# Block attention into a softplus feed-forward: m-tiles of four token tiles instead of three, attention two tiles at a time

## The chip, the core and the metric

The kernel runs on one core of one Trainium2 chip. The time is the device time of one execution in microseconds (us); lower is better. PE is TensorE (its weight loads are shown as PEld), DVE is VectorE, ACT is ScalarE, POOL is GpSimd, and SP is SyncE, which here only issues DMAs. Every engine works through its own instructions in order and waits on semaphores for the others.

## What is computed

Attention within chunks of 64 positions (8 batches, 8 heads, 576 positions, 64 dimensions a head), and on its result, as 4608 tokens of 512 features, a feed-forward layer with softplus and 2048 hidden features:

```python
def _attn_ref(q, k, v):
    B, H, S, D = q.shape
    chunk = 64
    nc = S // chunk
    q_c, k_c, v_c = (t.reshape(B, H, nc, chunk, D) for t in (q, k, v))
    scores = 1.0 / np.sqrt(D) * np.matmul(q_c, k_c.transpose(0, 1, 2, 4, 3))
    scores = scores - np.max(scores, axis=-1, keepdims=True)
    attn = np.exp(scores)
    attn = attn / (np.sum(attn, axis=-1, keepdims=True) + 1e-09)
    return np.matmul(attn, v_c).reshape(B, H, S, D).astype(np.float32)

def _moe_ref(x, w_in, w_out):
    h = x @ w_in
    g = np.maximum(h, 0.0) + np.log1p(np.exp(-np.abs(h)))
    return (g @ w_out).astype(np.float32)
```

The feed-forward's weights come as 64-bit floats, the rest as 32-bit.

## The kernel before

**Tiles.** A token tile is 128 tokens (two chunks, all heads); there are 36. An m-tile is TPM = 3 of them. The hidden features are FC = 16 chunks of 128. A *block* is one m-tile with one chunk: G1 (`gemm1`, L517) multiplies x by a chunk of w_in into PSUM (`ph`), softplus follows on ACT (`sp_g`), and G2 (`gemm2`, L552) multiplies the result by a chunk of w_out and adds it up over the chunks in one PSUM bank (`po`) for each token tile. There are 12 m-tiles, so 192 blocks. Every factor is split into a high and a low part in a format that PE multiplies in one pass, and three products stand for one: G1 has 12 matmuls of 384 columns, G2 9 of 512. `sp_hi` (ACT) and `sp_lo` (DVE) split the softplus; x is split by `att_xh` and `att_xl`.

**Weights.** A *unit* is one chunk of w_in or w_out, 32 in all. Each is loaded as 512 KB of 64-bit floats (`w_load`) and built up from integer halves: `w_top` and `w_low` on ACT, `w_sign` on POOL, `w_shift` and `w_add` on DVE, then the high part (`w_hi`: ACT for w_in, POOL for w_out) and the low part (`w_lo`: DVE for w_in, POOL for w_out and for two units of `LO_POOL`). The first 12 units use 8 places in the space of the second half of w_in, the later ones 3 buffers for the top and 2 for the low part. Three raw buffers take the loads, and the outputs too.

**Order of the m-tiles.** The list `phases` splits the first m-tile: its chunks 0 to 7, then the whole second m-tile, then its chunks 8 to 15. The partial sums of the first half wait in SBUF (`pp`).

**Attention.** Tiles 0 to 5 go one way (T, S, E, V: PE transposes q and k, multiplies, transposes the weights of attention, multiplies by v), tiles 6 to 35 another: q and k are loaded in blocks of 32, transposed by DVE (`blk_t`), and S of tile i and V of tile i - 1 run in one *burst* on PE (`burst`, L509) between a G1 and a G2; DVE, ACT and eight DMAs within SBUF (`blk_swap`) turn the weights of attention in between. Each such tile has 8 DMAs for q, 8 for k, 4 for v and 8 for the swap, all issued by SP. There is one buffer each for q, k, v and the transposed tiles, and one PSUM slot of two banks (`pa`) for bursts.

**Order.** All of it is tasks of a planner (class `Plan`): each has an engine, a cost, the tasks that it needs, an urgency (lower goes first) and the buffers that it takes. The planner runs them through and emits the instructions in that order. G1 and G2 stand in a fixed sequence: G1 of block g, then G2 of block g - LAG, LAG = 2. `BEGIN` lists the first bursts by block. `keep_warm` puts multiplications of the identity where the planner sees a gap of PE before 90 us.

PSUM has 8 banks: 3 `po`, 3 `ph`, 2 for `pa`.

Of the kernel before, what the change touches and what calls it, by code (L numbers as in the profile page):

```python
# [32 lines left out]
class Plan:  # L33
# [12 lines left out]
    def add(self, name, eng, cost, fn, needs=(), urg=0.0, table=None, take=(), kb=0, slack=0.0, after=()):  # L46
        self.tasks[name] = dict(
            name=name, eng=eng, cost=cost, fn=fn, needs=list(needs) + list(after), after=set(after), urg=urg, table=table,
            take=take, kb=kb, slack=slack, seq=len(self.tasks),
        )  # L50

    def order(self):
# [6 lines left out]
        fin, issued, free, tab, dma_free = {}, {}, {}, None, 0.0  # L59
# [29 lines left out]
        while times:  # L89
# [3 lines left out]
            for eng in list(wait):  # L93
# [13 lines left out]
                end = now + cost  # L107
                free[eng] = end
# [26 lines left out]
def chunked_attention_softplus_ffn(  # L135
# [19 lines left out]
    TPM = 3  # L155
# [5 lines left out]
    LAG = 2  # L161
    HALF_FC = 8
    FIRST_BLK = 6
    UW = 512
    RAW_BUFS = 3
    TOP_BUFS = 3
    LOW_BUFS = 2
    FILL = 0.6
# [26 lines left out]
    xs = [  # L195
        tuple(xpool.tile([P, 2 * TPM, KC, C], F32R, name=f"x_{part}{j}") for part in ("hi", "lo"))
        for j in range(2)
    ]

    def x_of(m):  # L200
        return xs[0] if m == 0 else xs[1] if m == 1 else xs[(m + 1) % 2]
# [66 lines left out]
    def w_hi(u, is_in, fc):  # L268
        t, hi, lo = w_parts(u, is_in, fc)
        if is_in:  # L270
            nc.scalar.copy(hi, t)
        else:
            nc.gpsimd.tensor_copy(hi, t)
# [6 lines left out]
    def slot(i, n):  # L280
        if ("slots", i) not in live:
            live["slots", i] = [late.tile([P, DM], F32, name="late") for _ in range(5)]
        return live["slots", i][n]

# [27 lines left out]
    def keep_warm(dst):  # L312
        for _ in range(int(FILL * plan.gap / 0.22)):
            nc.tensor.matmul(dst[:, :P], ident, ident, start=True, stop=True)
        plan.gap = 0.0
# [4 lines left out]
    def pe_t(i):  # L320
        if i < TPM:
            tq, tk = (ps_o.tile([P, DM], F32, name="po") for _ in range(2))
            keep_warm(tq)
        else:
            pa = pa_tile()
            tq, tk = pa[:, 0, :], pa[:, 1, :]
            keep_warm(tq)
# [15 lines left out]
    def pe_s(i):  # L343
        qT, kT = (slot(i, n).rearrange("p (a t) -> p a t", a=HP) for n in (3, 4))
        if i < TPM:
            sc = ps_h.tile([P, 512], F32, name="ph")
            keep_warm(sc)
        else:
            sc = pa_tile()[:, 0, :]
            keep_warm(sc)  # L350
# [12 lines left out]
    def pe_e(i):  # L363
        if i < TPM:
            tp = ps_h.tile([P, 512], F32, name="ph")
            keep_warm(tp)
        else:
            tp = pa_tile()[:, 0, :]
            keep_warm(tp)
# [7 lines left out]
    def pe_v(i):  # L377
        eT, vt = slot(i, 1).rearrange("p (a t) -> p a t", a=HP), hd(slot(i, 2))
        xp = pa_tile()
        keep_warm(xp[:, 0, :])  # L380
        for hp in range(HP):
            for h2 in range(2):
                for c2 in range(2):
# [3 lines left out]
                        xp[o, c2, hp * C : (hp + 1) * C],  # L387
# [5 lines left out]
        live["xp", i] = xp[:, :, : HP * C].rearrange("p c (a t) -> p c a t", t=C)  # L393


    def blk_load(i, name, src):
        dst = ld.tile([P, H, 2, BL], F32, name=name)
# [50 lines left out]
    def blk_v_load(i):  # L448
        v_load(i, ld.tile([P, H * D], F32, name="v"))
# [96 lines left out]
    def sp_lo(w):  # L546
        w["lo"] = g_tile(w, "g_lo")
        nc.vector.tensor_tensor(w["lo"], w["u"], w["hi"].bitcast(F32), op=ALU.subtract)  # L548
# [3 lines left out]
    def gemm2(w):  # L552
        if w["first"]:
            pos[w["ph_no"]] = [ps_o.tile([P, DM], F32, name="po") for _ in range(TPM)]
        g_hi, g_lo, fc = w["hi"], w["lo"], w["fc"]
        w_hi_, w_lo_ = wo[fc]
        if w["first"]:
            keep_warm(pos[w["ph_no"]][0])
        for t in range(TPM):
            ts_ = slice(t * P, (t + 1) * P)  # L560
            for n, (gg, wt) in enumerate(((g_lo, w_hi_), (g_hi, w_lo_), (g_hi, w_hi_))):
                nc.tensor.matmul(  # L562
                    pos[w["ph_no"]][t], gg[:, ts_], wt,
# [3 lines left out]
    parts = {}  # L567

    def evacuate(w, t):
        m, po = w["m"], pos[w["ph_no"]][t]  # L570
        done = w["fc"] == FC - 1
        if done:
            o = ld.tile([P, 2 * UW], I32, name="raw", bufs=RAW_BUFS)[:, :DM].bitcast(F32)
        else:
            o = parts[m, t] = pp.tile([P, DM], F32, name="part")
        if done and (m, t) in parts:
            nc.vector.scalar_tensor_tensor(
                o, po, 1.0 / WSCALE, parts[m, t], op0=ALU.mult, op1=ALU.add
            )
        else:  # L580
            nc.scalar.activation(o, po, AF.Copy, scale=1.0 / WSCALE)  # L581
        live["o", m, t] = o
# [32 lines left out]
    def due(g):
# [3 lines left out]
    units = sorted(  # L619
        [(first_use[fc], 1, fc) for fc in range(FC)] + [(first_use[fc] + 1.5, 0, fc) for fc in range(FC)]  # L620
    )
    of_in, of_out = {}, {}
    for u, (g, is_in, fc) in enumerate(units):
# [4 lines left out]
        if not is_in and fc >= HALF_FC:  # L628
            for j in range(2 * (fc - HALF_FC), min(2 * (fc - HALF_FC) + 2, LATE)):
                users.append("EVVSS"[j % 5] + str(j // 5 + FIRST_BLK - TPM))  # L630
        pl = "DVE" if is_in and u not in LO_POOL else "POOL"
# [167 lines left out]
```

## Time and profile before

| | us |
|---|---|
| median of 3 runs | 901.97 (900.75 to 903.83) |
| profiled execution | 899.45 |
| its span | 897.7 |
| PE busy | 881.9 |
| ACT busy | 392.8 |
| DVE busy | 354.7 |
| POOL busy | 66.8 |
| first G1 starts | 29.41 |
| last matmul ends | 894.02 |

The span is the time from the first to the last instruction that the profiler recorded on the core. In the profile, a line such as L527 is a line of the kernel printed above: L527 are the matmuls of G1, L562 those of G2, L423 and L491 the S and V of the bursts. Waits are put down to the instruction that ended last before the waiting one ran.

### The profile page before, as it was taken

To read this page: it belongs to the slowest core of one execution; us is meant where nothing else is said; L and a number is where in the kernel's file an instruction comes from. 1 tells how busy PE (TensorE), PEld (TensorE's weight loads), DVE (VectorE), ACT (ScalarE), POOL (GpSimd) and SP (SyncE) were. 2 spreads that over 40 slices of the span, in tenths; PEclk is the share of its full clock that TensorE was granted. 3 is DMA by queue.
4 is the path that set the end of the run, shared out by engine and by line. 5 is a ranking of instruction groups with operands and counts; after the bars stand their busy time and mean duration, and the time that the engine had idled before them with its cause. 6 is when DMAs were issued, how large, how long until landed. Compare 5 with 4: busy or idle time off the path is not lost.

```text
span 897.7 us, 16500 instructions
## 1 busy us (share of the span) xinstructions
PE 881.9 (98%) x6490; PEld 789.6 (88%) x6490; DVE 354.7 (40%) x616; ACT 392.8 (44%) x653; POOL 66.8 (7%) x72
## 2 busy tenths in 40 slices
PE   7988999999999999999999999999999999999998
PEld 7877988898898888888888888889889888888997
DVE  4898764233333333333333332332333333331110
ACT  5887556333343343334334334333334334332222
POOL 2656531000000000000000000000000000000000
PEclk9999999999999999999999999999999999999999
DMA  9945552332232223223222222223223222110000
GB/s 241 246 137 176 117 127 62 90 78 48 48 83 48 49 51 71 48 49 74 45 50 72 48 48 69 46 52 76 48 49 83 48 48 48 60 25 1 36 1 35
DMA packets 209501, 63.50 MB, mean 71 GB/s; under 512 B 186896, under 2 KB 202768, under 8 KB 209424
## 3 DMA queue, kind: packets, MB, share of 16 engines
q1 hardware_dynamic: 209424, 62.45, 30.0%
q8 instruction: 51, 0.84, 0.4%
q14 instruction: 26, 0.21, 0.1%
HBM read 45.09 MB, written 9.44 MB: 61 GB/s over the span
## 4 chain that ended last, share of the span: by engine, by line
PE 89%; SPq 4%; ACT 2%; DVE 2%; DMA 2%; issue 1%; POOL 1%; DVEq 0%; ACTq 0%
PE po L562 43%; PE ph L527 42%; PE pa L491 2%; PE pa L423 2%; DMA raw<-in_moe_w_in_dram 1%; SPq L297 1%; SPq L445 1%; SPq L404 1%; SPq L306 0%; DVE top L249 0%; DVE wib L249 0%; DVE top L245 0%; DVE wi_lo L277 0%; DMA v<-in_v_dram 0%; ACT L540 0%
## 5 line engine op out<-in xcount | busy, mean ns | idle before, releaser
L548 DVE TENSOR_TENSOR g_lo<-u,g_hi 128x384 fp32r<-128x384 f32 x191 | 108.1, 566 | 471.4 <-ACT g_hi L544 471.2
L540 ACT ACTIVATE u<-ph 128x384 f32<-128x384 f32 x192 | 94.3, 491 | 398.8 <-PE ph L527 396.2
L527 PE MATMUL ph<-x_hi,wib 128*128 128x384 f32 x768 | 213.1, 338 | 0.0
L562 PE MATMUL po<-late,g_hi 128*128 128x512 f32 x537 | 171.3, 395 | 0.0
L527 PEld LDWEIGHTS ph<-x_hi,wib 128*128 128x128 f32 x768 | 140.4, 188 | 4.1
L527 PE MATMUL ph<-x_hi,wi_lo 128*128 128x384 f32 x384 | 130.3, 339 | 1.0 <-DVE wi_lo L277 1.0
L527 PE MATMUL ph<-x_lo,wi_hi 128*128 128x384 f32 x384 | 129.1, 336 | 2.3 <-DVE x_lo L507 2.3
L527 PE MATMUL ph<-x_hi,wi_hi 128*128 128x384 f32 x384 | 129.7, 338 | 0.0
L527 PE MATMUL ph<-x_lo,wib 128*128 128x384 f32 x384 | 129.0, 336 | 0.0
L562 PEld LDWEIGHTS po<-late,g_hi 128*128 128x128 f32 x537 | 100.9, 188 | 20.0
L562 PE MATMUL po<-wo_hi,g_lo 128*128 128x512 f32 x288 | 115.8, 402 | 0.0
L562 PE MATMUL po<-wo_hi,g_hi 128*128 128x512 f32 x288 | 114.1, 396 | 0.0
L562 PE MATMUL po<-late,g_lo 128*128 128x512 f32 x285 | 113.6, 398 | 0.0
L562 PE MATMUL po<-wo_lo,g_hi 128*128 128x512 f32 x288 | 113.3, 393 | 0.0
L544 ACT CAST g_hi<-u 128x384 fp32r<-128x384 f32 x191 | 98.2, 514 | 5.6
L527 PEld LDWEIGHTS ph<-x_lo,wi_hi 128*128 128x128 f32 x384 | 72.1, 188 | 6.5 <-DVE x_lo L507 2.5
L527 PEld LDWEIGHTS ph<-x_hi,wi_lo 128*128 128x128 f32 x384 | 72.1, 188 | 5.2 <-DVE wi_lo L277 1.3
L527 PEld LDWEIGHTS ph<-x_lo,wib 128*128 128x128 f32 x384 | 72.1, 188 | 4.3
L527 PEld LDWEIGHTS ph<-x_hi,wi_hi 128*128 128x128 f32 x384 | 72.0, 188 | 0.0
L562 PEld LDWEIGHTS po<-wo_hi,g_hi 128*128 128x128 f32 x288 | 54.1, 188 | 12.6
L562 PEld LDWEIGHTS po<-wo_hi,g_lo 128*128 128x128 f32 x288 | 54.4, 189 | 10.0 <-ACT part L581 0.2
L562 PEld LDWEIGHTS po<-late,g_lo 128*128 128x128 f32 x285 | 53.9, 189 | 9.4
(94 smaller groups left out, 766.5 us busy)
## 6 DMA issues: line engine op xcount, KB each, us to landing
out_dram<-raw SPq DMA_DIRECT2D x36, 256.0 KB, 2.3
raw<-in_moe_w_in_dram SPq DMA_DIRECT2D x16, 512.0 KB, 4.4
raw<-in_moe_w_out_dram SPq DMA_DIRECT2D x16, 512.0 KB, 4.0
q<-in_q_dram SPq DMA_DIRECT2D x240, 32.0 KB, 2.1
k<-in_k_dram SPq DMA_DIRECT2D x240, 32.0 KB, 2.1
v<-in_v_dram SPq DMA_DIRECT2D x120, 64.0 KB, 2.4
eT<-eA SPq DMA_DIRECT2D x240, 32.0 KB, 1.8
late<-in_q_dram SPq DMA_DIRECT2D x5, 256.0 KB, 4.8
```

The lines of the kernel that those rows point to most:

```text
L297: eng.dma_start(dst[p0 : p0 + rows], src[b, :, s0 : s0 + rows, :].rearrange("h s d -> s h d"))
L404: nc.sync.dma_start(dst[p : p + BL, :, tb, :], src[b, :, s0 : s0 + BL, dh * BL : (dh + 1) * BL].rearrange("h s d -> s h d"),)
L423: nc.tensor.matmul(pa[o, c2, col : col + C], qT[r, a * HP + hl, :], kT[r, a * HP + hl, :], start=True, stop=True,)
L445: nc.sync.dma_start(eT[d : d + BL, tb], ea[s : s + BL, kb])
L491: nc.tensor.matmul(pa[o, a, col : col + C], vt[r, 4 * j + 2 * h2 + c2, :], eT(r, c2, j, h2), start=True, stop=True,)
L527: nc.tensor.matmul(ph, wt[:, c, fs], x[:, :, c, :], start=(n == 0), stop=(n == 3 * KC - 1))
L540: nc.scalar.activation(w["u"], w["ph"], AF.Softplus)
L544: nc.scalar.copy(w["hi"], w["u"])
L548: nc.vector.tensor_tensor(w["lo"], w["u"], w["hi"].bitcast(F32), op=ALU.subtract)
L562: nc.tensor.matmul(pos[w["ph_no"]][t], gg[:, ts_], wt, start=(w["first"] and n == 0), stop=(w["last"] and n == 2),)
```

## The change

- An m-tile has four token tiles (TPM = 4): nine m-tiles, 144 blocks, G1 and G2 of 12 matmuls of 512 columns each. The first m-tile is no longer split; `phases`, `pp` and the partial sums go. LAG is 1.
- PSUM is divided anew: 4 `po`, and 2 slots of two banks (`pa`) that G1 and bursts share; `ph` goes. T, S and E of the first tiles use `po`.
- Tiles 0 to 3 go the first way, ahead of G1; tiles 4 to 35 go by bursts, two tiles to a burst (two halves, each with its own PSUM slot): 17 bursts, at blocks 2, 10 and 15 and from then on at block 6 and 13 of each m-tile. q and k of a pair share their load buffers with v; the transposed q and k share space with the weights of attention.
- Early loads (part of tile 3, and q, k, v of tiles 4 to 7) lie in the space that x of the second m-tile takes later (`early`).
- All weight loads come after v of tile 3 (`LOAD_AFTER`). There are 2 buffers for top instead of 3. Which unit's high and low parts are made on POOL is listed (`HI_POOL`: 18 units, `LO_POOL`: 6), as is `sp_lo` of eight blocks (`GLO_POOL`) and the norm of tiles 0, 6 and 7 (`NORM_POOL`); the planner takes POOL and two steps of DVE to use one port.
- From the burst at block 15 on, exponentials come after the next block's `sp_hi`. Outputs are copied alternately by ACT and DVE, two to a raw buffer.

```diff
-    TPM = 3
+    TPM = 4
-    LAG = 2
+    LAG = 1
-    FIRST_BLK = 6
+    FIRST_BLK = 4
-    TOP_BUFS = 3
+    TOP_BUFS = 2
...
-    ps_h = ctx.enter_context(tc.tile_pool(name="ps_h", bufs=3, space=PSUM))
-    ps_a = ctx.enter_context(tc.tile_pool(name="ps_a", bufs=1, space=PSUM))
+    ps_a = ctx.enter_context(tc.tile_pool(name="ps_a", bufs=2, space=PSUM))
...
+    early = [xpool.tile([P, TPM, DM], F32, name="x") for _ in range(2)]
+    xs = []
     def x_of(m):
-        return xs[0] if m == 0 else xs[1] if m == 1 else xs[(m + 1) % 2]
+        while len(xs) <= min(m, 1):
+            xs.append([xpool.tile([P, 2 * TPM, KC, C], F32R, name="x") for _ in range(2)])
+        return xs[m % 2]
+
+    def early_slot(n):
+        return early[n // TPM][:, n % TPM, :]
...
     def w_hi(u, is_in, fc):
         t, hi, lo = w_parts(u, is_in, fc)
-        if is_in:
-            nc.scalar.copy(hi, t)
-        else:
-            nc.gpsimd.tensor_copy(hi, t)
+        nc.gpsimd.tensor_copy(hi, t) if u in HI_POOL else nc.scalar.copy(hi, t)
...
     def blk_load(i, name, src):
-        dst = ld.tile([P, H, 2, BL], F32, name=name)
+        if i in (FIRST_BLK + 1, FIRST_BLK + 3):
+            dst = early_slot(2 * (i - FIRST_BLK) + "qk".index(name))
+        else:
+            dst = ld.tile([P, DM], F32, name=name)
...
     def blk_v_load(i):
-        v_load(i, ld.tile([P, H * D], F32, name="v"))
+        v_load(i, early_slot(i % 2 + 4) if i < FIRST_BLK + 2 else ld.tile([P, DM], F32, name="qk"[i % 2]))
...
-    def burst(iv, i_s):
+    def burst(p_v, p_s, n):
         pa = pa_tile()
-        if iv is not None:
-            blk_v(iv, pa)
-        if i_s is not None:
-            blk_s(i_s, pa)
+        if p_v is not None:
+            blk_v(2 * p_v + n, pa)
+        if p_s is not None:
+            blk_s(2 * p_s + n, pa)

     def gemm1(w):
         x_hi, x_lo = x_of(w["m"])
-        ph = ps_h.tile([P, 512], F32, name="ph")[:, :MT]
+        ph = pa_tile()[:, 0, :MT]
...
-    def sp_lo(w):
+    def sp_lo(w, pool):
         w["lo"] = g_tile(w, "g_lo")
-        nc.vector.tensor_tensor(w["lo"], w["u"], w["hi"].bitcast(F32), op=ALU.subtract)
+        (nc.gpsimd if pool else nc.vector).tensor_tensor(w["lo"], w["u"], w["hi"].bitcast(F32), op=ALU.subtract)
...
+    HI_POOL = (1,2,3,5,7,8,9,12,15,19,21,22,24,25,28,29,30,31)
+    LOAD_AFTER = "v3"
+    LO_POOL = (2,6,8,22,23,26)
+    NORM_POOL = (0,6,7)
+    GLO_POOL = (2,3,5,7,8,10,14,15)
+    BEGIN = (2, 10, 15)
+    BURST_AT = (6, 13)
+    QK_AFTER = "v3"
+    EXP_FROM = 2
-    phases = [(0, range(HALF_FC)), (1, range(FC)), (0, range(HALF_FC, FC))]
-    phases += [(m, range(FC)) for m in range(2, NM)]
...
+            plan.add(f"B{at}_{n}", "PE", (0.5 if pv is None or ps is None else 0.94) + 0.36 * (n == 0), partial(burst, pv, ps, n),
+                     [f"G1_{at}" if n == 0 else f"B{at}_0"] + needs, urg=-10, take=[("pa", rel)])
...
+        for i in (a, b):
+            for n, src in (("q", q), ("k", k)):
+                if ps == F or i == FIRST_BLK + 3:
+                    free = []
+                elif i == b:
+                    free = [f"T{n}{a}"]
+                else:
+                    free = [f"T{n}{a - 2}" if ps <= F + 2 else f"B{prev}_{'qk'.index(n)}"]
+                plan.add(f"{n}{i}", "SP", 4.0, partial(blk_load, i, n, src), free, urg=d - QK_URG, kb=256,
+                         after=[QK_AFTER])
+                keep = [f"S{FIRST_BLK - 1}"] if ps == F else [f"Te{i - 2}" if n == "q" else f"swap{i - 2}"]
+                plan.add(f"T{n}{i}", "DVE", 0.65, partial(blk_t, i, n), [f"{n}{i}"] + keep, urg=d - T_URG)
+        nxt = [f"T{n}{b + 2 - 2 * (ps == NPT // 2 - 1)}" for n in "qk"]
...
+            plan.add(f"v{i}", "SP", 2.0, partial(blk_v_load, i), free, urg=d - V_URG, kb=256,
+                     after=[QK_AFTER])
...
+            plan.add(f"exp{i}", "ACT", 0.58, partial(att_exp, i), [f"sub{b}"], urg=d, table="exp",
+                     after=[f"hi{at + 1}"] if ps >= F + EXP_FROM and at + 1 < NG else [])
...
         seq.append(f"G1_{g}")
+        seq += [f"B{g}_{n}" for n in range(2) if g in bursts]
```

More of the change, by code (lines that the diff above doesn't have):

```diff
@@ L107, in order @@
                 end = now + cost
+                if t["port"]:
+                    end = port = max(now, port) + cost
                 free[eng] = end
@@ L320, in pe_t @@
     def pe_t(i):
[L321 to L327, printed above, removed]
+        tq, tk = (ps_o.tile([P, DM], F32, name="po") for _ in range(2))
+        keep_warm(tq)
         for dst, n in ((tq, 0), (tk, 1)):
@@ L363, in pe_e @@
     def pe_e(i):
[L364 to L369, printed above, removed]
+        tp = ps_o.tile([P, DM], F32, name="po")
+        keep_warm(tp)
         for hp in range(HP):
@@ L629, in chunked_attention_softplus_ffn @@
             for j in range(2 * (fc - HALF_FC), min(2 * (fc - HALF_FC) + 2, LATE)):
-                users.append("EVVSS"[j % 5] + str(j // 5 + FIRST_BLK - TPM))
-        pl = "DVE" if is_in and u not in LO_POOL else "POOL"
+                users.append("EVVSS"[j % 5] + str(j // 5))
+        pl = "POOL" if u in LO_POOL else "DVE"
+        ph_ = "POOL" if u in HI_POOL else "ACT"
         staged = u < STAGED
-        plan.add(f"load{u}", "SP", 0.6, partial(w_load, u, is_in, fc), urg=d - 6 if u else LQ, kb=512,
-                 take=[("raw", [f"w_top{u}", f"w_low{u}"])], after=["k1"])
+        plan.add(f"load{u}", "SP", 0.6, partial(w_load, u, is_in, fc), urg=d - LEAD if u else LQ, kb=490,
+                 take=[("raw", [f"w_top{u}", f"w_low{u}"])], after=[LOAD_AFTER])
@@ L648, in chunked_attention_softplus_ffn @@
-        plan.add(last[1], pl, 1.35 if pl == "POOL" else 0.7, partial(w_lo, u, is_in, fc, pl == "POOL"), [last[0]] + users, urg=d + 2.8)
-    def chain(i, d, kw):
+        plan.add(f"w_sign{u}", "POOL", 0.77, partial(w_sign, u), [f"w_low{u}"], urg=d + 0.5)
+        plan.add(f"w_shift{u}", "DVE", 0.42, partial(w_shift, u), [f"w_sign{u}"], urg=d + 0.7, port=True)
+        plan.add(f"w_add{u}", "DVE", 0.68, partial(w_add, u), [f"w_shift{u}", f"w_low{u}"], urg=d + 1.4, port=True)
+        freed = []
@@ new lines, in chunked_attention_softplus_ffn @@
+        if is_in and fc == HALF_FC:
+            freed = [f"w_{n}{j}" for n in ("hi", "lo") for j in range(STAGED)]
+        if fc:
+            freed.append(f"w_hi{(of_in if is_in else of_out)[fc - 1]}")
+        plan.add(last[0], ph_, 0.65 if ph_ == "POOL" else 0.53, partial(w_hi, u, is_in, fc),
+                 [f"w_add{u}"] + users + freed, urg=d + 2.1)
+        plan.add(last[1], pl, 1.3 if pl == "POOL" else 0.65, partial(w_lo, u, is_in, fc, pl == "POOL"),
+                 [last[0]] + users, urg=d + 2.8)
@@ new lines, in chunked_attention_softplus_ffn @@
+    for i in range(FIRST_BLK):
+        d, kw = -60 + 3 * i, KS
+        two = 2 * i // NCH != (2 * i + 1) // NCH
+        for pl, (n, src) in enumerate((("q", q), ("k", k), ("v", v))):
+            plan.add(f"{n}{i}", "SP", 0.6 * (1 + two), partial(pe_load, nc.sync, i, src, pl),
+                     urg=VQ + i if pl == 2 else d - 6 + 0.1 * pl, kb=310,
+                     after=[f"q{i}"] if pl else [f"q{i - 1}"] if i else [])
+        plan.add(f"T{i}", "PE", 1.1, partial(pe_t, i), [f"q{i}", f"k{i}"], urg=d,
+                 take=[("po", [f"tq{i}"]), ("po", [f"tk{i}"])])
+        plan.add(f"tq{i}", "ACT", 0.58, partial(pe_tq, i), [f"T{i}"], urg=d + 1 * kw)
+        plan.add(f"tk{i}", "DVE" if i in TK else "ACT", 0.60, partial(pe_tk, i), [f"T{i}"], urg=d + 1 * kw)
+        plan.add(f"S{i}", "PE", 1.45, partial(pe_s, i), [f"tq{i}", f"tk{i}"], urg=d + 2 * kw,
+                 take=[("po", [f"sub{i}"])])
```

279 lines of the change are left out of this document (113 added, 166 removed).

## The prediction

> **What bounds the kernel now.** I read the page first: its busy times, then the slices.
>
> ```profile
> span 897.7 us, 16500 instructions
> PE 881.9 (98%) x6490; PEld 789.6 (88%) x6490; DVE 354.7 (40%) x616; ACT 392.8 (44%) x653; POOL 66.8 (7%) x72
> ...
> PE   7988999999999999999999999999999999999998
> ...
> DVE  4898764233333333333333332332333333331110
> ```
>
> TensorE (PE) is busy almost throughout. Only the first four slices (22.4 us each) have holes, and there VectorE (DVE) is at 0.8 to 0.9. So there are two questions: does the change alter PE's work, and does it alter the first 110 us? The chain of waits gives the steady pace:
>
> ```profile
> 183.21 2.11 PE ph L527 x12
> 187.41 2.11 PE ph L527 x12
> ...
> 203.22 2.30 PE po L562 x9
> ...
> 225.51 2.30 PE po L562 x9
> ```
>
> A block (one G1, one G2) takes 187.41 - 183.21 = 4.20 us. From one burst's G2 to the next are 22.29 us, which is five blocks (21.0) and a burst of 1.29.
>
> The timeline of PE shows single matmuls and the inside of a burst:
>
> ```profile
> 29.84 0.34 PE L527 MATMUL ph<-x_hi,wi_hi 128*128 128x384 f32 x1
> ...
> 31.23 0.33 PE L527 MATMUL ph<-x_lo,wi_hi 128*128 128x384 f32 x1
> ...
> 39.65 0.39 PE L562 MATMUL po<-wo_hi,g_hi 128*128 128x512 f32 x1
> ...
> 41.04 0.40 PE L562 MATMUL po<-wo_hi,g_hi 128*128 128x512 f32 x1
> ...
> 202.05 0.69 PE L491 MATMUL pa<-eT,v 64*64 64x64 f32 x32
> 202.57 0.65 PE L423 MATMUL pa<-kT,qT 64*64 64x64 f32 x32
> 203.15 0.51 PE L562 MATMUL po<-wo_hi,g_lo 128*128 128x512 f32 x1
> ```
>
> Eight 384-column matmuls start within 1.39 us, 0.174 each; six of 512 within 1.39, 0.232 each. Both are 2.21 columns per ns: time goes by columns, and nothing worth counting goes per matmul. In the burst the V half takes 0.52, the S half 0.58; the other 0.2 of the 1.29 is the change of shape on both sides.
>
> The first phase, from the first G1 at 29.41 until the matmuls run without a hole at 80.60, is a stretch of the windows view; two of its waits are from PE's timeline:
>
> ```profile
> 29.41:80.60 51.19, 45.69 (x410) 39.80 (x409) 44.80 (x67) 42.69 (x74) 29.35 (x31) 1.00 0.60 182
> ...
> 59.72 0.94 PE L314 MATMUL pa<-ident 128*128 128x128 f32 x6 [1.57 <-ACT late L375]
> ...
> 76.50 0.44 PE L527 MATMUL ph<-x_lo,wi_hi 128*128 128x384 f32 x1 [2.26 <-DVE x_lo L507]
> ```
>
> Its columns are PE, weight loads, DVE, ScalarE (ACT) and GpSimd (POOL). In these 51.19 us PE runs nine G1 and seven G2: 16 x 2.10 = 33.6. So 17.6 us are something else: a few waits like the two shown (together about 5.5), and about 12 us of attention of tiles 3 to 5 with the identity fillers between. Account of before: 29.4 start, 806.3 blocks (192 x 4.20), 39.7 bursts (28 x 1.29 and four of one half at about 0.8), 17.6 first phase, 3.7 tail, 1 left over: 897.7.
>
> **The change, part by part.**
>
> *Blocks.* 192 blocks of 9,216 columns become 144 of 12,288: the same columns. A new block is 24 x 0.232 = 5.56, and 0.03 of change of shape as now: 5.59. 144 x 5.59 = **805.0**, 1 us less.
>
> *Bursts.* 31 slots for single tiles become 17 for pairs: 15 full, one S only, one V only. The second tile adds 2 x 0.52, its change of shape being paid already: 1.29 + 1.04 = 2.33. 15 x 2.33 + 2 x 1.3 = **37.6**, 2 less, though two more tiles (4 and 5) go this way.
>
> *First phase.* Tiles 4 and 5 leave the T, S, E, V path, tile 3 moves ahead of the first G1: the 12 us go, and so do the 5.5 of waits with the places they stood at. What is late instead is below.
>
> *Start.* Four tiles come ahead of G1, and the weight loads behind all their q, k and v.
>
> ```profile
> 11.84 1.86 SPq L211 DMA_DIRECT2D raw<-in_moe_w_in_dram  x1
> ...
> 10.40 0.69 DVE L455 TENSOR_REDUCE mx<-ph 128x8 f32<-128x512 f32 x1 [1.84 <-PE ph L357]
> ...
> 17.12 0.67 ACT L227 ACTIVATE wib<-raw 128x512 f32<-128x512 f32 x1 [0.93 <-DMA raw<-in_moe_w_in_dram]
> ...
> 26.87 0.69 DVE L507 TENSOR_TENSOR x_lo<-pa,x_hi 128x512 fp32r<-128x512 f32 x1 [0.61 <-ACT x_hi L503]
> ```
>
> Before, x of tile 2 is done at 27.56 and G1 starts at 29.41, after a T of tile 3. By 11.84 SyncE had issued ten tile loads and one weight load of twice the size. That is the new twelve, so the first weight load lands near 17.1, where the second one did, and with 5 to 7 us of steps its unit is ready by 24. Tile 3's q and k land where tile 2's did (the weight load ahead of them is gone). From the first maximum at 10.40 DVE has five and a half instructions of 0.69 for each of four tiles, 15 us, without the weights of before in between; the end of the last tile's way to x, in which engines wait for one another, I put at 1 to 5 us more: 26 to 30. I take **28**.
>
> *Weights in the first m-tile.* Now 32 units must be ready within 16 blocks instead of 16 and later 16. A unit costs, by the answers for its lines (min/median/max):
>
> ```profile
> L241 POOL CAST wib<-wib x12: 759/960/1240, 10.5 to 50.5; 128x512 f16<-128x512 f32 x12
> ...
> L245 DVE TENSOR_SCALAR top<-top x20: 411/434/1471, 53.6 to 141.3; 128x512 int32<-128x512 int32 x20
> ...
> L249 DVE CUSTOM_DVE_ANT_0 top<-top,low x16: 680/786/1664, 62.6 to 106.6; 128x1024 uint16<-128x1024 uint16 x16
> L249 DVE CUSTOM_DVE_ANT_0 wib<-wib x8: 679/840/1205, 30.6 to 53.0; 128x1024 uint16<-128x1024 uint16 x8
> ...
> L273 POOL CAST wo_hi<-wib x5: 609/745/1014, 27.3 to 53.1; 128x512 fp32r<-128x512 f32 x5
> ...
> L277 DVE TENSOR_TENSOR wib<-top,wib x8: 672/688/1196, 76.9 to 126.8; 128x512 fp32r<-128x512 f32 x8
> ...
> L277 POOL TENSOR_TENSOR late<-top,late x7: 1275/1341/1608, 81.5 to 129.7; 128x512 fp32r<-128x512 f32 x7
> ...
> L507 DVE TENSOR_TENSOR x_lo<-pa,x_hi x7: 653/691/693, 20.0 to 149.9; 128x512 fp32r<-128x512 f32 x7
> ...
> L548 DVE TENSOR_TENSOR g_lo<-u,g_hi x25: 517/558/1535, 34.6 to 148.8; 128x384 fp32r<-128x384 f32 x25
> ```
>
> First bound, by the pace reached: from 30.6 to 106.6 before made 24 adds, one per unit: 76.0 / 23 = 3.30 us a unit. The new order wants two per block of 5.59, with its share of bursts (6 us over 16 blocks) 2.98 a unit. The first add can come near 20; the last, 31 x 3.30 later, at 122, its parts ready near 125. Without a hole the last G2 of m-tile 0 would start at 28 + 16 G1 and 15 G2 (86.7) + the next G1 (2.8) + bursts (6.0) = 123.5. So 1 to 2 us late.
>
> Second bound, by the work: the two engines get in each other's way. Beside POOL, an instruction of DVE takes longer:
>
> ```profile
> 39.80 1.53 DVE L548 TENSOR_TENSOR g_lo<-u,g_hi 128x384 fp32r<-128x384 f32 x1
> ...
> 39.62 1.30 POOL L277 TENSOR_TENSOR wo_lo<-wib,wo_hi 128x512 fp32r<-128x512 f32 x1
> ```
>
> 1.53 beside the POOL instruction, 0.56 as a median. Shift, add, lo and g_lo have such long ones, up to 1.2 to 1.7 in the rows above; x_lo, which reads PSUM, has none (at most 0.69). With the shortest durations, POOL gets 32 x 0.76 + 18 hi x 0.61 + 6 lo x 1.28 + 8 g_lo x 1.28 + 2 norm x 1.28 = 56 us; DVE's instructions that lengthen are 32 x (0.41 + 0.68) + 26 lo x 0.67 + 8 g_lo x 0.69 (0.52 x 512/384) + 2 norm x 0.67 = 59. In series 115, less some 0.08 that neighbours overlap (166 x 0.08 = 13): 102, and a third to a half of DVE's other 25 us (some 35 instructions like x_lo: 12 transposes, and maximum, subtraction, sum and second transpose of four tiles) finds no cover: 111 to 115. From 19 on that ends at 130 to 134, 7 to 11 late. Were the two engines independent, DVE alone (84) would be ready in time.
>
> The Trainium skill says, in "SBUF — State Buffer", section "Who interferes with whom", that DVE and POOL share one port pair under an exclusive lock: the second to issue waits for the whole instruction. That speaks against moving 18 hi, 8 g_lo and the norms to POOL: by it the sum is the serial one, by independent engines there is no hole. The row at 39.80 agrees with the lock.
>
> *SyncE.* A third bound is the chain between two bursts of the first m-tile, at blocks 10 and 15:
>
> ```profile
> 273.91 3.25 SPq L306 DMA_DIRECT2D v<-in_v_dram  x4
> 277.25 4.00 SPq L404 DMA_DIRECT2D q<-in_q_dram  x8
> 281.35 3.85 SPq L404 DMA_DIRECT2D k<-in_k_dram  x8
> 285.30 5.01 SPq L445 DMA_DIRECT2D eT<-eA  x8
> ...
> eT<-eA SPq DMA_DIRECT2D x240, 32.0 KB, 1.8
> ```
>
> The queue is in order. After block 10's burst the scores of tiles 6 and 7 need about 11 us to their transposes; then two swaps (10.0), q and k of tile 9 (7.9), its transposes, v of 6 and 7 (about 5.5 for both, without waits), and about 2 to land: 36. Five blocks and the burst give 30.3. That is about 5 late if nothing else is, and it overlaps with the lateness above. I take **8** for all holes of the first m-tile, between 1 and 16.
>
> *Edits costed at nothing.* By the groups of ACT:
>
> ```profile
> L540 ACT ACTIVATE u<-ph 128x384 f32<-128x384 f32 x192 | 94.3, 491 | 398.8 <-PE ph L527 396.2 <-DVE g_lo L548 2.1
> ...
> L540 ACT ACT_TABLE_LOAD x32 | 41.1, 1283 | 7.3 <-PE ph L527 4.1
> ```
>
> G1 and bursts now share two PSUM slots. The second burst half needs the softplus of the G1 before it, 0.65 (0.49 x 512/384) after that G1, and the first half (1.3) covers it; the next G1 needs sub and x_lo of the first tile, about 4.9 after (four DVE instructions of 0.7 and the ACT steps), covered by both halves and a G2 (5.1). If this cover goes, it is some 0.3 x 15. With one G2 of lag instead of two, softplus, hi and lo (2.0, with a table load of 1.28 3.3) lie under G2 and the next G1 (5.6). Outputs are copied on two engines, under the last G2 and the next G1.
>
> *Sum.* 28 + 805.0 + 37.6 + 8 + 3.7 tail = **882.3** span, against 897.7. The profiled execution took 899.45 in all, 1.75 beyond its span, and the median 901.97 is 2.5 above it: 882.3 + 1.75 + 2.5 = 886.6, say **887**.
>
> **Rivals.**
>
> A: the weights keep up, no hole in m-tile 0 (0 to 3 us). For it: the pace of 3.30 was reached with three full tiles in between and 2.98 is near; against: in those 51 us DVE and POOL are busy for 44.8 and 29.4, which in series is more than there is, and PE waited for them. About 880.
>
> B: the shared work is heavier, 16 to 25 us of holes: four startup tiles keep DVE until 27, so the lead is gone, and SyncE issues some 100 us of loads in that phase, weights behind q and k. 895 to 904.
>
> C, slower than before: the chain between bursts is late at every seven-block distance, eight of them to the end. Exponentials now wait for the next block's hi (9 us after G1), so the transposes end at 15; two swaps 10.0, q and k 7.9, v 5, landing and transposes: 40.5 to the last v, against 7 x 5.59 + 2.33 = 41.5, and 42.8 for its half. Eight times its lateness is added: it decides from a chain of about 45 us, 2.2 late each, 18 in all: 905 and above. Against: the cover holds with 2 to spare, and loads land in 2 us at this load. For: issue is 100% in order.
>
> D: the early loads in x's space do not come early, because 16-engine DMA is full until 40 us (3.1 MB of tiles, 1.5 MB of weights ahead of them): the burst at block 2 waits some 5 us. It is within the forecast's holes.
>
> **How the numbers follow.** The forecast (holes of 3 to 16 us, with D) has 0.57: 882 to 895. A has 0.15, B 0.14, C 0.14 (half of it between 893 and 905). A measurement tells 0.3% (2.7 us) from no change. Faster by more: all of A and the forecast, 0.08 of B, 0.04 of C: 0.84. Same: 0.08. Slower: 0.08. The range reaches from A's 878 into B, 901.
>
> **What would show it.** Right: blocks of 5.59 and bursts of 2.33 with no wait in the steady part; first G1 near 28; holes only ahead of 135 us, ended by wi_lo, wo_lo, x_lo or by DMA of v and swaps; DVE and POOL full from 20 to 125. Wrong: a pace per 512 columns above 0.232, a G1 after a burst that waits for sub or x_lo, or waits of PE on DMA at blocks 13 of later m-tiles.

## The result and the profile after

The changed kernel takes 915.41 us (914.13 to 916.18) against 902.9 of the kernel before beside it: a ratio of 1.0139, with a 95% interval of 1.0113 to 1.0165. It is 1.4% slower, where 887 was forecast.

The page of after, its head and the slices of 22.8 us, beside the lines shown of before (PEclk is the clock that PE was granted, in tenths of full speed):

```profile
span 912.4 us, 14898 instructions
...
PE 876.0 (96%) x5878; PEld 710.3 (78%) x5878; DVE 347.0 (38%) x590; ACT 323.0 (35%) x501; POOL 61.8 (7%) x73
...
PE   8499979999999999999999999999999997999998
...
DVE  5478866442423352234323442334143413112111
...
PEclk9799999999999999999999999999999998999999
```

PE's holes are in the first six slices, 137 us (before: the first four, 90 us), and there is a new one in slice 34. The chain of waits of after in the steady part (start, duration, what):

```profile
186.40 2.75 PE pa L528 x12
189.15 0.62 PE pa L492 x32
...
191.20 2.98 PE po L561 x12
...
194.19 2.99 PE pa L528 x12
197.18 2.80 PE po L561 x12
...
205.53 2.76 PE pa L528 x12
208.28 2.80 PE po L561 x12
211.08 2.76 PE pa L528 x12
```

A block takes 211.08 - 205.53 = 5.55 (forecast 5.59); from 186.40 to 199.97 are two blocks and a burst, so the burst is 13.57 - 11.10 = 2.47 (2.33). The steady part came as forecast, and after the first m-tile only one long wait stands in PE's timeline:

```profile
757.75 1.41 PE L492 MATMUL pa<-eT,k 64*64 64x64 f32 x10 [4.85 <-DMA k<-in_v_dram]
```

The rest is ahead of 156 us. PE's timeline there (in brackets: idle time before, and what ended it):

```profile
27.52 0.69 PE L383 MATMUL pa<-x,eT 64*64 64x64 f32 x32 [0.68 <-ACT x L371]
...
38.49 0.80 PE L528 MATMUL pa<-x,wi_lo 128*128 128x512 f32 x1 [8.97 <-ACT x L504]
...
73.42 0.50 PE L528 MATMUL pa<-x,wi_lo 128*128 128x512 f32 x1 [1.90 <-DVE wi_lo L279]
112.13 3.01 PE L528 MATMUL pa<-x,wib 128*128 128x512 f32 x12 [1.14 <-DVE wib L279]
121.25 4.61 PE L528 MATMUL pa<-x,wib 128*128 128x512 f32 x12 [3.32 <-POOL wib L279]
...
137.94 4.42 PE L528 MATMUL pa<-x,wib 128*128 128x512 f32 x12 [3.22 <-DVE wib L279]
...
155.92 0.40 PE L561 MATMUL po<-wo_end,g_hi 128*128 128x512 f32 x1
```

The first G1 starts at 38.49 (forecast 28); long waits are ended by the low parts of w_in; the last row is the second matmul of the last G2 of the first m-tile, which so starts at 155.7. The forecast had it at 123.5 + 8 = 131.5. That is 24.2 late; the wait at 757 and the slow matmuls behind it cost 8.4 more, the 13 full bursts behind it 13 x 0.14 = 1.8, and 128 shorter blocks give back 128 x 0.04 = 5.1: together 29.3 of the 30.1 between 882.3 and 912.4.

Why the first G1 is late stands in the timelines of SyncE's queue and of ACT:

```profile
16.79 7.22 SPq L315 DMA_DIRECT2D x<-in_v_dram  x8
24.05 4.05 SPq L405 DMA_DIRECT2D q<-in_q_dram  x8
28.15 3.91 SPq L405 DMA_DIRECT2D k<-in_k_dram  x8
32.18 1.65 SPq L216 DMA_DIRECT2D raw<-in_moe_w_in_dram  x1
```

```profile
37.30 0.67 ACT L232 ACTIVATE wib<-raw 128x512 f32<-128x512 f32 x1 [9.83 <-DMA raw<-in_moe_w_in_dram]
37.87 0.57 ACT L504 CAST x<-pa 128x512 fp32r<-128x512 f32 x1
```

V of tile 3 ends at 28.2 (L383 above), but its x_hi (L504) stands on ACT behind w_top of the fourth weight unit, and that unit's load behind v of tiles 4 and 5 and q and k of tile 4 on SyncE.

### The profile page after: what moved, and what is told of

Read it like the earlier page. It is cut to its first block, busy times and chain, and to the rows that moved or that the text cites. A ratio compares the mean times of both kernels' runs of the same rounds, so it can differ in the third digit from the quotient of the medians.

```text
span 912.4 us, 14898 instructions
## 1 busy us (share of the span) xinstructions
PE 876.0 (96%) x5878; PEld 710.3 (78%) x5878; DVE 347.0 (38%) x590; ACT 323.0 (35%) x501; POOL 61.8 (7%) x73
## 4 chain that ended last, share of the span: by engine, by line
PE 87%; DMA 4%; SPq 4%; ACT 2%; DVE 2%; issue 1%; POOL 0%; ACTq 0%
PE po L561 42%; PE pa L528 41%; DMA raw<-in_moe_w_in_dram 2%; PE pa L492 2%; SPq L405 2%; DMA raw<-in_moe_w_out_dram 2%; PE pa L425 1%; SPq L306 1%; DMA x<-in_q_dram 1%; SPq L446 1%; SPq L216 0%; DVE top L254 0%; ACT u L539 0%; ACT top L232 0%; DMA k<-in_v_dram 0%
## 5 line engine op out<-in xcount | busy, mean ns | idle before, releaser
L539 ACT ACTIVATE u<-pa 128x512 f32<-128x512 f32 x144 | 86.0, 597 | 514.1 <-PE pa L528 508.6
L528 PE MATMUL pa<-x,wib 128*128 128x512 f32 x864 | 213.9, 397 | 7.7 <-DVE wib L279 4.4
L547 DVE TENSOR_TENSOR g_lo<-u,g_hi 128x512 fp32r<-128x512 f32 x136 | 93.0, 684 | 304.0 <-ACT g_hi L543 304.0
L528 PEld LDWEIGHTS pa<-x,wib 128*128 128x128 f32 x864 | 163.4, 190 | 47.8 <-POOL wib L279 3.8
L528 PE MATMUL pa<-x,wi_hi 128*128 128x512 f32 x576 | 181.4, 397 | 0.0
L528 PEld LDWEIGHTS pa<-x,wi_hi 128*128 128x128 f32 x576 | 110.0, 191 | 25.5 <-DVE x L508 0.4
L528 PE MATMUL pa<-x,wi_lo 128*128 128x512 f32 x288 | 115.6, 401 | 10.9 <-ACT x L504 9.0
L543 ACT CAST g_hi<-u 128x512 fp32r<-128x512 f32 x144 | 89.3, 620 | 4.3
L528 PEld LDWEIGHTS pa<-x,wi_lo 128*128 128x128 f32 x288 | 54.9, 191 | 24.7 <-ACT x L504 9.2
L561 PEld LDWEIGHTS po<-wo_lo,g_hi 128*128 128x128 f32 x288 | 54.7, 190 | 12.1
L413 DVE STREAM_TRANSPOSE ka<-k 128x512 f32<-128x512 f32 x30 | 21.3, 711 | 53.4 <-DMA k<-in_k_dram 38.4
```

The source lines that it names most:

```text
L528: nc.tensor.matmul(ph, wt[:, c, fs], x[:, :, c, :], start=(n == 0), stop=(n == 3 * KC - 1))
L539: nc.scalar.activation(w["u"], w["ph"], AF.Softplus)
L543: nc.scalar.copy(w["hi"], w["u"])
L547: (nc.gpsimd if pool else nc.vector).tensor_tensor(w["lo"], w["u"], w["hi"].bitcast(F32), op=ALU.subtract)
L561: nc.tensor.matmul(pos[w["m"]][t], gg[:, ts_], wt, start=(w["first"] and n == 0), stop=(w["last"] and n == 2),)
```

## The experiments

A number for all of them: from the start of that last G2 to the end of the span are 756.7 us in the changed kernel. Where the wait at 757 is gone it is 747.4 to 749.3 in all eleven runs. So a run's time is told by when its first m-tile ends ("last G2" below). Behind a run's time stand, in brackets, its ratio to the kernel before and the 95% interval. Each edit also gives the planner new costs or conditions, so the order of other tasks can move with it. "On e1" means with e1's edit in place.

**The wait at 757.** Loads of v for tile 34 stand ahead of those for tile 33 on SyncE, and wait there for the burst at block 118 to free their buffer; the second half of that burst needs tile 33. SyncE's queue shows the stop as one long row (v of tiles 32 and 34), with v of tile 33 behind it:

```profile
733.17 21.90 SPq L315 DMA_DIRECT2D q<-in_v_dram  x8
755.11 2.59 SPq L315 DMA_DIRECT2D k<-in_v_dram  x4
```

Edit:

```diff
-            free = [] if ps == F else [nxt[n]]
+            free = [] if ps == F else [f"B{at}_{n}"] if ps == NPT // 2 - 1 else [nxt[n]]
```

> The v loads of the last pair (tiles 34 and 35) are given the burst at block 118 as what they wait for, so that they no longer stand in SyncE's queue ahead of the load of v of tile 33. Theory Q (a wait in the in-order DMA queue, plus TensorE's clock that falls in the hole): the hole of 5 us after 752 us goes and with it the 3 us of slow matmuls behind it, about 8 us off the span of the changed kernel, 912.4 to about 904. Rival: the hole only covers another one (the next burst, seven blocks on, then waits for its swap or v instead): within 3 us of 912.

906.26, ratio 1.0038 (1.0023 to 1.0053), span 904.3: 8.1 less, as theory Q has it, and the wait is gone. It is still not faster than the kernel before.

**An earlier start.** First by ACT's order, then by the order of the loads:

```diff
-        plan.add(f"w_top{u}", "ACT", 0.58, partial(w_top, u), [f"load{u}"], urg=d,
+        plan.add(f"w_top{u}", "ACT", 0.58, partial(w_top, u), [f"load{u}"], urg=d, after=[f"xl{FIRST_BLK - 1}"] if u >= 3 else [],
```

```diff
-    BEGIN = (2, 10, 15)
+    BEGIN = (4, 10, 15)
-    QK_AFTER = "v3"
+    QK_AFTER = "load4"
```

The first edit is e2's, which also puts the transposes of tiles 4 and 5 behind x of tile 3; the second is e3's.

> On ScalarE and VectorE the x of tile 3 goes ahead of the first steps of weight unit 3 and of the transposes of tiles 4 and 5, no DMA is moved. Rival S (the late start is simply added to the time): first G1 near 30 instead of 38.5, and the span shorter by 9 to 12 us, 901 to 904. Theory W (the weight units bound the first m-tile, and they flow late because their loads stand behind tile loads in SyncE's queue): first G1 near 30 too, but the last G2 of m-tile 0 hardly earlier than 155.7; the gain at the start comes back as holes, and the span is within 5 us of 912.

> The loads of q, k, v of tiles 4 and 5 go behind weight load 4 in SyncE's queue, and their burst is at block 4 instead of 2; the order on ScalarE is left to the planner. Theory W: the fourth weight load is issued near 20 us instead of 32, VectorE and GpSimd have weight work from 25 on, the first G1 is near 29, and the last G2 of m-tile 0 starts at 135 to 145 instead of 155.7: span 895 to 902. Rival S: the same gain as in the run with x of tile 3 first, no more: 901 to 904.

Both start near 30 and end later: e2 918.09 (1.0166, 1.0142 to 1.0191), last G2 at 157.9; e3 917.44 (1.0158, 1.014 to 1.0176), last G2 at 158.7. Theory W holds for e2, but for e3 it had the last G2 at 135 to 145; rival S misses both. The time won comes back as waits for weights. PE of e2, then of e3, each with its longest wait:

```profile
41.36 0.77 PE L528 MATMUL pa<-x,wi_lo 128*128 128x512 f32 x1 [7.87 <-DVE wi_lo L279]
```

```profile
91.18 5.19 PE L528 MATMUL pa<-x,wib 128*128 128x512 f32 x12 [6.56 <-DVE wib L279]
```

In e2 the fourth load is still issued at 33.6. In e3 it is issued at 21.4, but later two swaps hold SyncE from 77.73 to 87.81, and DVE stands at the transpose of what they carry, ahead of the low part that PE waits for:

```profile
89.51 0.71 DVE L413 STREAM_TRANSPOSE ka<-x 128x512 f32<-128x512 f32 x1 [3.33 <-DMA eT<-ka]
```

**Three other suspects.** e4 takes the low parts of the softplus off POOL (`GLO_POOL = ()`). e5 (on e1) puts identity matmuls ahead of five G1, so that PE's clock stays up in the waits:

```diff
+        for _ in range(WARM.get(w["g"], 0)):
+            nc.tensor.matmul(ph[:, :P], ident, ident, start=True, stop=True)
```

e7 (on e1) gives the planner SyncE's measured costs (tile load 1.05, v 2.7, swap 5.0 in place of 0.6, 2.0, 3.2).

> All low parts of the softplus are made on VectorE, none on GpSimd. Theory P (from 50 us on VectorE and GpSimd in series, sharing a port, are the limit): eight instructions of 1.28 become eight of 0.69, 5 us less of serial work, and the first m-tile ends 0 to 5 us earlier. If the two were independent, VectorE alone would get 5.5 us more and the stage would end up to 5 us later. If SyncE's queue alone decided: no change of the end beyond 1 us.

> Beside the last pair's v loads in order (span 904.3 without this): 34, 8, 3, 12 and 12 multiplications of the identity are put ahead of G1 of blocks 0, 5, 11, 12 and 14, where TensorE waits; each takes about 0.22 us and they fit into the holes. Theory K (TensorE's clock, at half speed behind a hole, is a cost of its own): the slow matmuls behind four holes (2.7, 1.7, 1.7 and 1.4 us above the steady pace) go, and the span is 5 to 8 us shorter, 896 to 899. Theory W (the weight units bound the first m-tile, TensorE's own speed there costs nothing): the holes grow by what the matmuls save, span within 2 us of 904.

> Beside the last pair's v loads in order (904.3 without this): the planner is given SyncE's issue times as the trace has them (first tile loads 1.05 instead of 0.6, v 2.7 instead of 2.0, swap 5.0 instead of 3.2), nothing else. If the wrong times made the order bad: weight load 3 stands ahead of k of tile 4, first G1 near 31, and the last G2 of m-tile 0 at 145 to 150, span 893 to 899. If the order is as good as it can be with one queue: within 3 us of 904. If the longer swaps make the planner move work behind them in the later m-tiles: slower, 905 to 920.

e4: 920.24 (1.0188, 1.0166 to 1.021), last G2 at 162.3, 6.6 later than in the changed kernel; none of the three expectations holds. From the first G1 to the last G2 the busy times of DVE and POOL add up to 135.7 us (141.2 in the changed kernel), DVE alone has 89.3 (85.9), and the m-tile takes 6.2 more. So less work of the two in sum did not end it sooner; whether DVE's share or the planner's new order made it later is not shown. e5: 905.72, clock 0.998, last G2 at 155.7 (155.9 in e1). Theory W holds: a slow clock in these waits costs nothing, since weights are waited for anyway. e7: 904.37, last G2 at 156.2: a plan with the measured costs for the same queue is worth 2 us of time at most (the intervals of e1 and e7 just touch), none of it in the first m-tile.

**Weight loads on ACT's queue** (on e1, from the fourth load on): `(nc.sync if u < RAW_BUFS else nc.scalar).dma_start`, each load behind the one before.

> Beside the last pair's v loads in order (904.3 without this): the weight loads from unit 3 on are issued by ScalarE instead of SyncE, so they don't stand behind tile loads and swaps. Theory W (late weight loads in SyncE's queue): the fourth load is issued near 21 us instead of 34, the first G1 is near 30, the slack of VectorE and GpSimd at 30 to 50 and at 130 to 140 fills, the last G2 of m-tile 0 starts at 135 to 145 instead of 155.9, span 884 to 894. Rival P (the serial work of VectorE and GpSimd and the chain of a unit through two buffers are the limit): first G1 near 30, but the last G2 of m-tile 0 not before 150, span 898 or more.

923.29 (1.0218, 1.0196 to 1.0239), last G2 at 172.4, 16.5 later than in e1. The fourth load is issued at 23.08 and the first G1 starts at 32.15, yet PE then waits longer. PE's longest wait, and DVE's timeline ahead of its end:

```profile
44.77 1.22 PE L528 MATMUL pa<-x,wi_hi 128*128 128x512 f32 x2 [12.13 <-DVE x L508]
```

```profile
38.46 0.71 DVE L413 STREAM_TRANSPOSE ka<-k 128x512 f32<-128x512 f32 x1 [7.85 <-DMA k<-in_k_dram]
...
42.49 0.71 DVE L413 STREAM_TRANSPOSE qe<-x 128x512 f32<-128x512 f32 x1 [3.02 <-DMA x<-in_k_dram]
...
44.03 0.68 DVE L508 TENSOR_TENSOR x<-pa,x 128x512 fp32r<-128x512 f32 x1
```

x_lo of tile 3 (L508) stands behind transposes of tiles 4 and 5 that wait for SyncE's loads: the queue was changed, and the next engine in order takes its place. Further waits, of 3.5 us at 81.95 and 3.9 at 135.21, make up much of the rest and were not followed up. Theory W falls; rival P's bounds (not before 150, 898 or more) hold, but neither named this wait.

**Two loads taken away, singly and together.** This settles it. On e1; e8 leaves out the three steps that add a weight's low bits, e9 makes each q, k and swap of tiles from 4 on one DMA of the same bytes, without the rearrangement; e10 is both. One line of each edit (w_sign and w_add go like w_shift, `blk_load` like the swap):

```diff
-        plan.add(f"w_shift{u}", "DVE", 0.42, partial(w_shift, u), [f"w_sign{u}"], urg=d + 0.7, port=True)
+        plan.add(f"w_shift{u}", "DVE", 0.01, lambda: None, [f"w_sign{u}"], urg=d + 0.7)
```

```diff
-                    nc.sync.dma_start(eT[d : d + BL, tb], ea[s : s + BL, kb])
+        nc.sync.dma_start(eT, ea)
```

> On top of the kernel with the two loads of v in their right order (906.3). It leaves out the three steps that add the low bits of each weight to its top part (the POOL cast, the shift and the add on DVE) for all 32 units; top, low, hi and lo stay, and every load stays. That takes 32 x (0.76 + 0.41 + 0.68) = 59 us of the 103 us of work of DVE and POOL off the first m-tile. Theory W (the first m-tile is bound by the work on DVE and POOL that a weight unit needs): the last G2 of the first m-tile starts 15 to 22 us sooner than 155.7, at 134 to 141, the holes of 1.9 to 3.3 us ended by wi_lo and wib go, 884 to 892 in all; the floor is the first G1 near 38 and 94.4 of PE work behind it. Rival Q (SyncE's queue in order is the bound: weight loads stand behind q, k and swaps): the holes stay and are ended by steps that wait for raw, 5 us at most, 901 to 906.

> On the same base. It leaves out the rearrangement of q and k of the tiles from 4 on and of the swaps: each of these loads is one DMA of the same bytes in place of eight, so SyncE issues for about 0.6 instead of 4.0 (q, k) and 5.1 (swap). The work of DVE and POOL is whole. Theory W: the start is sooner (the two loads ahead of the fourth weight unit fall from 8 to 1.2 us, first G1 30 to 33), and this is given back as holes ended by wi_lo and wib between 60 and 150; the last G2 of the first m-tile starts at 148 to 155, 899 to 906 in all. Rival Q: it starts at 134 to 141, 884 to 892.

> Both edits in one. Theory W and rival Q both give the floor: first G1 30 to 33, no hole over 1 us behind it, last G2 of the first m-tile at 125 to 130, 874 to 882 in all. If the steady rows are right as well, this is what the change was worth with its first m-tile not held up: the predicted 882.3 of span less the 8 of holes. If it stays above 890, something else than these two holds the first m-tile.

| on e1 | first G1 | last G2 | us |
|---|---|---|---|
| e1 | 39.8 | 155.9 | 906.26 |
| e8: less work on DVE, POOL | 38.4 | 153.2 | 904.04 |
| e9: fewer issues on SyncE | 29.4 | 143.9 | 894.57 |
| e10: both | 28.2 | 126.9 | 878.83 |

Ratios: 1.0009 (0.9998 to 1.002), 0.9911 (0.9889 to 0.9934), 0.9731 (0.9716 to 0.9745). 59 us less work for DVE and POOL are worth 2.2, fewer issues 11.7, both 27.4, almost twice the sum: each hides the other. W misses e8, whose time is Q's; both miss e9, which lies between them; e10's last G2 and time are as both said, though it keeps one wait of 2.38 us, for x_lo at 31.11. The stretch from the first G1 to the last G2 in the windows view (length, then busy PE, PEld, DVE, ACT, POOL, clock, DMA share, GB/s), for the changed kernel, e8, e9 and e10:

```profile
38.49:155.67 117.18, 105.34 (x716) 83.49 (x717) 85.90 (x136) 73.85 (x115) 55.29 (x61) 0.93 0.59 163
```

```profile
38.44:153.24 114.80, 104.10 (x708) 81.91 (x709) 46.81 (x77) 72.08 (x115) 29.31 (x31) 0.93 0.63 168
```

```profile
29.35:143.91 114.56, 100.48 (x718) 77.35 (x716) 92.41 (x140) 73.24 (x116) 60.12 (x63) 1.00 0.52 168
```

```profile
28.23:126.91 98.68, 95.89 (x711) 77.55 (x709) 48.60 (x79) 74.11 (x118) 30.40 (x31) 1.00 0.63 199
```

In e8 DVE and POOL are more than half idle, and the m-tile is as long as in e9. What it waits for at its end, on PE and on SyncE's queue:

```profile
137.11 0.29 PE L492 MATMUL pa<-eT,q 64*64 64x64 f32 x2 [1.31 <-DMA q<-in_v_dram]
...
144.09 1.15 PE L492 MATMUL pa<-eT,k 64*64 64x64 f32 x27 [1.97 <-DMA k<-in_v_dram]
```

```profile
112.74 10.98 SPq L446 DMA_DIRECT2D eT<-ka  x16
...
124.87 4.84 SPq L405 DMA_DIRECT2D q<-in_q_dram  x8
...
130.59 3.82 SPq L405 DMA_DIRECT2D k<-in_k_dram  x8
134.51 2.67 SPq L315 DMA_DIRECT2D q<-in_v_dram  x4
...
138.01 2.58 SPq L315 DMA_DIRECT2D k<-in_v_dram  x4
```

That is the chain of the prediction's third bound: two swaps, q, k, two v, from 112.74 to 140.59, and the burst at block 15 waits for the last v. From the G1 of block 15 to the next G1, e8 takes 17.72 us and e10 7.76 (PE's timelines, e8 first):

```profile
132.79 3.01 PE L528 MATMUL pa<-x,wib 128*128 128x512 f32 x12
...
150.51 0.39 PE L528 MATMUL pa<-x,wi_lo 128*128 128x512 f32 x1
```

```profile
116.42 2.91 PE L518 MATMUL pa<-x,wib 128*128 128x512 f32 x12
...
124.18 0.39 PE L518 MATMUL pa<-x,wi_lo 128*128 128x512 f32 x1
```

So 10.0 of e8's lateness arises here. Part of it is PE's clock: from 139 to 149 the granted clock is 0.51, and the G2 at 146.13 takes 4.38 in place of 2.80.

With SyncE alone in the way the last G2 is 26.3 us behind e10's (153.2 against 126.9), with DVE and POOL alone 17.0, with both 29.0: the larger bound nearly covers the smaller. In e9 the bound is DVE and POOL: from the first add at 22.9 to the last high part at 141.9, one of DVE and POOL is busy in 111.0 of 119.0 us (the union of their rows). In the changed kernel itself, from 22 to the last G2, it is 114.5 of 133.7, and SyncE 99.3.

One more thing changes in e9: its DMAs move the same bytes in 77,056 packets instead of 214,784. For the start the changed kernel points to the issuing and not to the transfers: from 20 to 40 us the DMA engines are busy for 0.60 of the time, while SyncE issues almost without a pause. Behind the start the two were not told apart.

**Which issues.** e11 makes only q and k of tiles 4 and 5 single DMAs, e12 only those from 6 on and the swaps.

> On the kernel with the two loads of v in their right order (906.3; first G1 at 39.8, last G2 of the first m-tile at 155.9). The rearrangement is left out for q and k of tiles 4 and 5 alone: each is one DMA, so SyncE has 4 x 3.4 us less to issue between 24 and 46. Theory Y (three bounds lie side by side in the first m-tile: SyncE's queue at its start, the work on DVE and POOL through its middle, SyncE's chain to the burst at block 15 at its end; one alone gives little): first G1 at 29 to 31, and of these 9 to 10 us at least half is given back, as holes ended by wi_lo and wib or by loads of v at block 15: last G2 at 150 to 156, 900 to 906 in all. Rival Z (all of the 11.7 us that the full cut of issues gained was the start): last G2 at 144 to 147, 895 to 898.

> On the same base, the other half of the cut: q and k from tile 6 on and all swaps are one DMA each; tiles 4 and 5 load as in the kernel. Theory Y: first G1 stays at 38 to 40; from there the work on DVE and POOL takes the 114.5 us that it took with the full cut, so the last G2 starts at 153 to 155 and the time is 903 to 906. Rival Z: no gain, the same numbers; rival V (the queue behind the start is the larger part): last G2 at 146 to 149, 896 to 900.

e11: 909.09 (1.0074, 1.0054 to 1.0093), first G1 29.3, last G2 158.1, outside what either theory said. e12: 900.44 (0.9969, 0.9956 to 0.9981), 38.9 and 150.8: more than Y expected, a little less than V, and not Z's "no gain". Together 3.0 won, against 11.7 in e9. SyncE's queue of e11 shows where the early part went:

```profile
26.09 5.37 SPq L411 DMA_DIRECT2D x<-in_q_dram  x8
31.50 3.90 SPq L411 DMA_DIRECT2D x<-in_k_dram  x8
35.52 0.39 SPq L216 DMA_DIRECT2D raw<-in_moe_w_in_dram  x1
```

The planner filled the freed queue with a later tile's q and k; the fourth weight load was issued at 35.5 all the same. e14 is e11 with the loads of tiles from 6 on behind weight load 4 (`after=[QK_AFTER if ps == F else "load4"]`); e13 does the same with nothing left out, and GpSimd issues q and k of tiles 4 and 5 (`nc.gpsimd if i < FIRST_BLK + 2 else nc.sync`).

> The run with one DMA each for q and k of tiles 4 and 5 gave nothing back: its freed queue was filled with q and k of tiles 6 and 7, and the fourth weight load was issued at 35.5 all the same. Here these loads of tiles from 6 on may only follow weight load 4 (counted from 0); all else as in that run (rearrangement of q and k of tiles 4 and 5 left out). Theory Y (weight loads standing behind q and k in SyncE's order are what the start costs, and the work on DVE and POOL is next): load 3 is issued by 27, the hole of 6.9 us before the first G2 goes, DVE and POOL are full from 30, and the last G2 of the first m-tile starts at 145 to 151, 896 to 902 in all. Rival P (DVE and POOL alone set the end wherever the loads stand): no sooner than 154, 904 and above.

> The same with nothing left out: q and k of tiles 4 and 5 stay rearranged, 32 DMAs, but GpSimd issues them from 5 us on instead of SyncE; loads of tiles from 6 on behind weight load 4. What an issue costs GpSimd no row shows; the plan counts 5.0 us for eight. Theory Y: if GpSimd is through with them before 25, the times of the run before (start near 30, last G2 at 145 to 153, 896 to 904). Rival G (issuing on GpSimd takes over a microsecond each, 32 us, and the casts of the first weight units stand behind it): first G1 at 42 or later, last G2 at 156 and above, 907 or more.

e14: 902.7 (0.9992, 0.9974 to 1.0009), load 3 issued at 26.6, first G1 28.7, last G2 150.6: as theory Y has it, the time 0.7 above its range; rival P falls. e13: 907.49 (1.0046, 1.003 to 1.0062), 34.9 and 156.1, no gain. Rival G has the last G2 and the time right, its price wrong. GpSimd's timeline has 0.58 for an issue:

```profile
14.16 4.62 POOL L405 DMA_DIRECT2D x<-in_q_dram  x8
```

But beside these transfers SyncE's loads of the first tiles take longer (1.14 for the last of them in the changed kernel, 2.42 here), the first weight load is issued at 17.32 instead of 13.10, and the start is late for that:

```profile
14.85 2.42 SPq L306 DMA_DIRECT2D eT<-in_v_dram  x1
```

No complete kernel beat the one before; the best, e7 at 904.37, is equal to it (1.001, 0.9995 to 1.0024).

## Why the prediction was wrong, by its steps

- **Blocks, bursts, tail.** Right: 5.55 for 5.59, 2.47 for 2.33. The cover of the G1 behind a burst is short by a little (2.99 for 2.76: 0.23, priced at 0.3). The account of before has a slip that enters no other term: 28 x 1.29 and four of 0.8 are 39.3, not 39.7.
- **Rivals C and D** did not come: SyncE's chain holds at seven blocks' distance, and the burst at block 2 waits 0.39 us, for a softplus.
- **Start: 28, was 38.5.** V of tile 3 ends at 28.2, so the way to there was right; x_lo comes later, and even in e10 the first G1 stands until 31.11 for it. The step that failed is "The weight loads behind all their q, k and v": it followed SyncE to 11.84 and x to its end, but not the next weight units. v of the pair (7.22 us) and q and k of tile 4 come between the third and the fourth weight load, and ACT's order puts that unit's w_top ahead of x_hi. Mending this alone wins nothing (e2, e3): the same queue is late again further on. A smaller slip: ahead of 11.84 SyncE had issued nine tile loads, not ten, so the first weight load came at 13.10 and was waited for until 19.05, not 17.1; no G1 waited for that.
- **Holes of the first m-tile: 8, was 21.7** (117.2 from first G1 to last G2, less the 95.5 that the forecast has without a hole). This is the term that decided. PE is idle in 11.8 of these 21.7 us; most of the rest are matmuls at the half rate behind the waits (granted clock 0.93 in this stretch), for which the forecast had no term. By e5 they only take the place of waits, so the two are one lateness. That the bounds overlap was right, as e8, e9 and e10 show; their sizes were not. The third bound, "about 5 late", took SyncE's chain between two bursts and left out what the queue has lost before it: with SyncE alone in the way (e8) it is 26.3 behind e10, of which 10.2 are the start, 10.0 the chain to block 15 and 6.1 lie between. The second was worked out at 111 to 115 us of work, and e9 has 111.0; but it begins at 22.9, not 19, and has 8 us of gaps, and comes out 17.0 behind e10, not 7 to 11 late.
- **Rival B** named the mechanism ("weights behind q and k") and priced its holes at 16 to 25; it had 0.14. It counted SyncE's "some 100 us of loads in that phase", and 99.3 were measured: that row was there and should have been carried through as a bound of its own. Its 895 to 904 still missed, by the start and by the 8.4 at 757, which no step looked for: the last pair's v was taken to load as every other pair's does.
- **Rival A**, no hole, 880: e10's span is 876.2. It leaves out work that the kernel before has too, so its 2.7% is not the worth of the change; it shows that the terms for PE were right.

What stays open: where the 6.1 us between the start and block 15 arise, and how SyncE's part divides in a complete kernel. e11, e12 and e14 move the start and the chain together, through the planner's order.

## What to carry to other kernels

Carry every bound through to the end of its phase: follow each in-order queue with every issue in it, not only the stretch in which it looked late, and for each late load ask what stands behind it on the engine that waits. Where two bounds lie close together, a cut of one shows only the distance to the next (2.2 us for 59 us of work), so cut both before either is called harmless.

## What was not expected of the hardware

In the changed kernel PE ran at the half rate behind waits as short as 1.90 us: the G1 at 73.42 takes 4.61 in the chain of waits. In PE's timeline above, the G1 behind waits of 3.32 and 3.22 take 4.61 and 4.42, and the one behind 1.14 takes 3.01. In e1 the G1 of the same block waits 2.26 us and then runs at full speed. The changed kernel's row, then e1's:

```profile
73.42 4.61 PE pa L528 x12
```

```profile
75.00 3.04 PE pa L528 x12
```

The Trainium skill, in "TensorE: Matmul & The Clock Gate", section "What's actually happening", has the clock fall after at least one idle window of about 3.4 us. The waits of 1.90, 3.22 and 3.32 us are shorter than that, and the half rate followed; behind 2.26 us it did not. So the length of the wait alone does not tell. In the first m-tile the half rate cost nothing (e5).

One DMA's issue held SyncE for 0.48 to 0.69 us in loads of q and k and in swaps (3.82 for eight, 10.98 for sixteen, in e8), and up to 2.42 in the start of e13, where GpSimd issues loads at the same time.
